# Softmax denominators gathered across four units, with a new written order, in an adaLN attention and token-MLP block

## The chip, the core and the metric

The kernel runs on one core of one Trainium2 chip. The engines that compute are PE (TensorE, matrix multiply into PSUM), DVE (VectorE), ACT (ScalarE) and POOL (GpSimd); SP (SyncE) issues nearly all DMA transfers here. The metric is device microseconds of one execution; a profile is one execution of its own, and its span runs from the first to the last instruction.

## What is computed

Two branches in a row over x (2048 tokens, 512 features), each behind a layer norm that is scaled and shifted by vectors made from a condition c. The first is attention with 32 heads of 16 features, causal, with a window of 256 keys. The second is an MLP that mixes tokens.

```python
mod = (_silu(c) @ w_mod).reshape(c.shape[0], 6, 1, -1)
sa, ca, ga, sb, cb, gb = (mod[:, i] for i in range(6))
h = _layernorm(x, axis=-1) * (1 + ca) + sa
x = x + ga * _A_ref(h, A_wqkv, A_wo)        # softmax(q k / 4, mask) v, then wo
h = _layernorm(x, axis=-1) * (1 + cb) + sb
x = x + gb * _B_ref(h, B_w1, B_b1, B_w2, B_b2)
# _B_ref: layernorm, gelu(w1^T h + b1) over tokens, then w2^T u + b2
```

## The kernel before

**Groups, units and chunks.** The 2048 tokens are worked in four groups G of 512, each of four tiles of 128. A *unit* is one set of eight heads (g8, of four) for 256 queries (H, of eight): 32 units. Their score blocks are packed into 75 *chunks*. A chunk is four strips of 512 columns: the score matmul S writes three strips to the PSUM tile `pss`, of which there is one, and one to `psb`, of which there are two; ACT takes two exponentials from them, the large EA (`et<-pss`, 128x1536) and the small EB (`et<-psb`, 128x512); DVE multiplies by the mask (M). When the last chunk of a unit is masked, the matmuls AV make values (`po[:,0]`) and, by a matrix of ones, sums (`po[:,1]`) in one PSUM bank. Each sum stands in the 16 partitions of its head. Groups 0 to 3 begin at chunks 0, 15, 35 and 55.

**After a unit** (`finish`, L1265): ACT takes the logarithm of the sums out of PSUM (ln), then the exponential of minus that (rz), both 128x256 and both into the tile `lz`; DVE multiplies values from PSUM by it into `OT`. The bank is free when that product is done.

**Work between the chunks.** Three PSUM banks ("od") are shared by AV and by all dense matmuls, which come in pieces of two 128x512 products: projections q, k, v of the next group (`proj`), the output projection wo, residual and second norm of the group before (`post`), and the first MLP product (`partials`: p for the first eight token tiles, p2 for four of them added later). ACT, DVE or POOL take the results out: ke, qe, ve copy projections from PSUM, kk, vo, vp lay out keys and values, n2, m2, hb make the second norm, pe and pd keep partial sums. When attention is over, `tail` ends the first MLP product (56 pieces u), with gelu (g), and last come 16 output tiles (`py`) of 14 products each.

**Order.** All of this is a list of 1165 operations. `ORDER` (L62) lists their numbers in the order in which they are written into the program, and so into each engine's queue; `CHOSEN` (L118) names the engine of those that can run on several. Each engine and SP work through their own queue in that order and wait for what an instruction needs. The costs in the code, such as 0.26 for ln, belong to the planner that made the order; the chip doesn't see them.

**DMAs in the middle.** SP issues xt (a transposing transfer of a normed tile into `h1T`, four to a group), vx (two transfers that swap halves of the values, `vs<-vb`), z2 (zeros for `VT`), and the weight loads w1a to w1d and w2, among others.

```python
ea = op("EA", "ACT", ..., deps=[s] + readers.get(i - E_BUFS, []), pos=i, cls="exp")
a = op("ln", "ACT", 0.26, e_ln, deps=[av], pos=i + LZ_POS)
b = op("rz", "ACT", 0.31, e_rz, deps=[a], pos=i + LZ_POS)
d = mult_ops[Hh, g8] = op("OT", "DVE", 0.34, e_o, deps=[b], pos=i + OT_POS)
unit["avs"][0].frees = [d]
```

Of the kernel before, what the change touches and what calls it, by code (L numbers as in the profile page):

```python
# [10 lines left out]
ALU = mybir.AluOpType  # L11
# [5 lines left out]
H = 32  # L17
# [42 lines left out]
E_BUFS = 7  # L60
LOG = None
ORDER = [  # L62
# [54 lines left out]
]  # L117
CHOSEN = {  # L118
    "ACT": [
        47, 48, 50, 51, 74, 82, 1062,  # L120
    ],
    "DVE": [
# [5 lines left out]
    ],  # L128
    "POOL": [
# [4 lines left out]
    ],  # L134
}
BATCH = True
XT_AFTER = -0.7
W1_AFTER = 2.0
AV_POS = 0.2
LZ_POS = 0.0  # L140
# [75 lines left out]
def kernel(  # L216
# [31 lines left out]
    class Ordered:  # L248
        def __init__(self, engine):
            self.engine = engine  # L250
# [1184 lines left out]
```

## Time and profile before

| | us |
|---|---|
| median of three runs | 253.65 (252.9 to 253.68) |
| span of the profiled execution | 252.3 |
| busy in it: PE, DVE, ACT, POOL | 235.3, 205.4, 179.5, 126.3 |
| granted TensorE clock, mean | 1.000 |

Nearly every operation is recorded at L256, the line of the wrapper that calls the engine, so groups are told apart by their tiles, not by lines. A row of groups gives count, busy time in us and mean duration in ns of one. ACT and DVE instructions overlap a little, so an instruction's duration is longer than its share of a full queue; that share is read from start to start. A table by stretches gives busy us and count of each engine.

### The profile page before, as it was taken

What the parts mean: (1) busy time and instruction counts of PE and PEld (TensorE: products, weight loads), DVE (VectorE), ACT (ScalarE), POOL (GpSimd) and SP (SyncE); (2) the same over time, 40 slices, a digit from 0 to 9 for tenths busy, and PEclk for the clock granted to TensorE, in tenths of its full rate; (3) what the DMA queues carried; (4) which work ended last, traced back from release to release, by engine and by line L of the source; (5) the groups of instructions that cost most, each with busy time, mean ns of one, the idle gap of its engine ahead of it and who ended that gap; (6) DMA issues with size and microseconds to landing.
All of it is one profiled execution on the core that took longest, in us unless ns stands there. A gap on an engine that the chain in (4) does not pass through costs nothing.

```text
span 252.3 us, 9189 instructions
## 1 busy us (share of the span) xinstructions
PE 235.3 (93%) x3949; PEld 126.0 (50%) x3949; DVE 205.4 (81%) x408; ACT 179.5 (71%) x254; POOL 126.3 (50%) x228
## 2 busy tenths in 40 slices
PE   7988888899987889999999999999999999999995
PEld 2656644445554544555546454556444444444443
DVE  5499998989989998999897999999978764444443
ACT  4699998999999999999999999997147510000000
POOL 8268968795899989845886348173000000000000
PEclk9999999999999999999999999999999999999999
DMA  6999364356055200003401536314999201111111
GB/s 200 323 351 294 48 47 86 44 70 187 3 74 112 53 23 3 4 3 104 131 3 45 155 82 189 105 44 113 343 388 386 108 22 43 44 52 52 42 44 42
DMA packets 42625, 28.13 MB, mean 111 GB/s; under 512 B 12376, under 2 KB 38488, under 8 KB 42584
## 3 DMA queue, kind: packets, MB, share of 16 engines
q1 hardware_dynamic: 42576, 27.54, 39.4%
q8 instruction: 31, 0.51, 0.9%
q14 instruction: 10, 0.08, 0.1%
q10 hardware_dynamic: 8, 0.00, 0.0%
HBM read 22.03 MB, written 2.10 MB: 96 GB/s over the span
## 4 chain that ended last, share of the span: by engine, by line
PE 52%; ACT 24%; DVE 7%; DMA 5%; issue 5%; POOL 4%; SPq 1%; POOLq 0%; DVEq 0%
ACT et L256 20%; PE py L256 19%; PE pu L256 16%; PE po L256 5%; PE pss L256 5%; ACT lz L256 3%; PE pa L256 3%; DMA x<-in_A_x_dram 2%; DVE et L256 2%; DMA h1T<-xn 2%; DMA wmod<-in_w_mod_dram 1%; POOL h1T L256 1%; PE pq L256 1%; DVE st L256 1%; PE pk L256 1%
## 5 line engine op out<-in xcount | busy, mean ns | idle before, releaser
L256 ACT ACTIVATE et<-pss 128x1536 bf16<-128x1536 f32 x75 | 110.7, 1476 | 2.8 <-PE psb L256 2.3
L256 PE MATMUL py<-guT,w2r 128*128 128x512 bf16 (+2 forms) x238 | 48.7, 366 | 0.0
L256 ACT ACTIVATE et<-psb 128x512 bf16<-128x512 f32 x75 | 46.9, 626 | 0.0
L256 DVE TENSOR_TENSOR et<-et,maskt 128x1024 bf16<-128x1024 bf16 (+2 forms) x79 | 46.4, 603 | 0.1
L256 PE MATMUL pu<-hb,w1s 128*32 128x512 bf16 (+1 forms) x302 | 39.0, 380 | 0.2 <-DVE QT L256 0.2
L256 PEld LDWEIGHTS <-w2r 128*128 128x128 bf16 x238 | 22.8, 98 | 26.1 <-issue 0.3
L256 PE MATMUL pss<-QT,KT 32*128 32x64 bf16 (+3 forms) x720 | 29.9, 230 | 6.2 <-ACT et L256 3.5
L256 PE MATMUL po<-et,VT 128*32 128x64 bf16 (+3 forms) x960 | 32.2, 234 | 1.3 <-DVE kb L256 0.6
L256 PE MATMUL po<-et,ones_bd 128*32 128x256 bf16 (+3 forms) x624 | 31.7, 268 | 0.0
L256 PEld LDWEIGHTS <-KT 32*128 32x128 bf16 x960 | 17.1, 92 | 28.5 <-issue 24.6
L256 DVE TENSOR_TENSOR otile<-py,xr 128x512 bf16<-128x512 f32 (+2 forms) x17 | 11.2, 660 | 24.4 <-PE py L256 24.2
L256 POOL TENSOR_SCALAR KT<-kb,mask_par 128x512 bf16<-128x512 bf16 (+1 forms) x36 | 25.0, 707 | 11.4 <-DVE kb L256 11.1
L256 PE MATMUL psb<-QT,KT 32*128 32x64 bf16 (+3 forms) x240 | 29.3, 231 | 0.0
L256 PEld LDWEIGHTS <-VT 128*32 128x32 bf16 x960 | 20.8, 96 | 13.2 <-issue 4.7
L256 PE MATMUL pk<-h1T,wqkv 128*32 128x512 bf16 (+4 forms) x228 | 21.1, 340 | 2.4 <-DVE OT L256 1.0
L256 DVE BATCH_NORM_STATS2 st<-x 128x6 f32<-128x512 bf16 x32 | 21.5, 680 | 2.1 <-DMA x<-in_A_x_dram 2.1
L256 PEld LDWEIGHTS <-wqkv 128*32 128x32 bf16 (+1 forms) x350 | 15.3, 96 | 12.7 <-issue 4.7
L256 PEld LDWEIGHTS <-w1s 128*32 128x32 bf16 (+1 forms) x302 | 14.1, 97 | 15.0 <-issue 1.5
L256 PE MATMUL pv<-wqkv,h1T 128*32 128x512 bf16 (+2 forms) x202 | 17.1, 348 | 1.3 <-DVE OT L256 0.7
L256 PE MATMUL pu<-hb,w1r 128*128 128x512 bf16 (+1 forms) x96 | 17.9, 380 | 0.0
L256 PE MATMUL pa<-wod,OT 128*32 128x512 bf16 (+1 forms) x136 | 17.2, 381 | 0.0
L256 PEld LDWEIGHTS <-ones_bd 128*32 128x32 bf16 x624 | 15.8, 97 | 0.1
(109 smaller groups left out, 350.1 us busy)
## 6 DMA issues: line engine op xcount, KB each, us to landing
w2r<-in_B_w_dram SPq DMA_DIRECT2D x14, 512.0 KB, 10.2
w1s<-in_B_w_dram SPq DMA_DIRECT2D x19, 256.0 KB, 4.0
w1r<-in_B_w_dram SPq DMA_DIRECT2D x9, 256.0 KB, 4.3
x<-in_A_x_dram SPq DMA_DIRECT2D x16, 128.0 KB, 5.2
wmod<-in_w_mod_dram SPq DMA_DIRECT2D x4, 512.0 KB, 7.8
out_dram<-otile SPq DMA_DIRECT2D x15, 128.0 KB, 1.7
wmod<-in_w_mod_dram SPq DMA_DIRECT2D x4, 256.0 KB, 3.9
wqkv<-in_A_wqkv_dram SPq DMA_DIRECT2D x4, 256.0 KB, 5.7
```

Source lines behind the costliest of these rows:

```text
L256: ins = call(*args, **kwargs)
```

## The change

**Sums (`finish`).** For 30 of the 32 units, values and sums are copied together from PSUM to an SBUF tile `ev` (128x512, f32, six of them) by DVE (26) or ACT (4); this copy frees the bank. A DMA (zg) then takes every eighth partition of the sums, 16 rows, to `zc`, where four units (two in the last batch) lie under one another. One ln and one rz, at most 64x256, serve the batch. A DMA for each unit (zb) spreads its 16 rows back over the 128 partitions of `ev`, and POOL (25) or DVE (5) multiplies values by it into `OT`. The last two units go as before, their lz in `ev`.

**Condition vectors.** The four vectors bc were made by 16 matmuls with 128 identical rows and taken out by four DVE instructions. Now 16 matmuls of 32 columns go side by side into one bank, one DVE instruction takes them out, and four DMAs (bb) spread them over the partitions.

**Written order.** On every engine each recorded instruction depends (without a semaphore) on the one before it, so none can change places where a pool is opened or closed. `ORDER` and `CHOSEN` are new, for 1206 operations; up to the first chunk the sequence is that of before with other numbers.

**Memory.** `et` has six buffers, not seven; the `work` pool is gone and its tiles are in `wpool`; `nothing` is in `modw`; the last four `hb` tiles are made after `wpool` is closed, and wait for it. Some costs of the planner are changed.

Counted by the numbers in the two orders, operations on each engine:

| | before | after |
|---|---|---|
| ln + rz on ACT | 32 + 32 | 10 + 10 |
| ev on DVE / ACT | none | 26 / 4 |
| OT on DVE / POOL | 32 / 0 | 7 / 25 |
| ve on DVE / ACT | 16 / 0 | 13 / 3 |
| pe on DVE / ACT | 13 / 1 | 10 / 4 |
| kk on DVE / POOL | 1 / 18 | 3 / 16 |
| vo on DVE / POOL | 2 / 10 | 0 / 12 |
| zg, zb, bb on SP | none | 30, 30, 4 |

```diff
-E_BUFS = 7
+E_BUFS = 6
+EV_BUFS = 6
 ORDER = [
...
                 if pinned[0]:
                     tc.keep_in_program_order(ins)
+                    if self.last is not None:
+                        tc.add_manual_dep(
+                            ins.ins, self.last, mybir.DependencyInfo(mybir.DependencyClass.NoSync, mybir.DependencyReason.DATA),
+                            reason="order",
+                        )
+                    self.last = ins.ins.name
...
+    def e_bc(n):
+        if n == 0:
+            box["bc"] = bank([P, D], F32, "ps_b")
+        for k in (2 * n, 2 * n + 1):
+            for i, (v, _) in enumerate(vectors):
                 te.matmul(
-                    box["bc", v][:], lhsT=sT_rep[:, k, :], rhs=wmod[:, k, v * D : (v + 1) * D],
-                    start=(k == 0), stop=(k == ND - 1),
+                    box["bc"][32 * i : 32 * i + 32, :], lhsT=sT_rep[:, k, :], rhs=wmod[:, k, v * D : (v + 1) * D],
+                    start=(k == 0), stop=(k == ND - 1), tile_position=(0, 32 * i), skip_group_check=True,
                 )
...
+    bce = op("bce", "DVE", 0.6, e_bce, deps=[bc_last], pos=9.0)
+    for n, (v, dst) in enumerate(vectors):
+        def e_bb(e, n=n, dst=dst):
+            dma.dma_start(out=dst[:], in_=bcs[32 * n : 32 * n + 32, :].unsqueeze(1).to_broadcast([32, ND, D]))
...
+        def e_ev(e):
+            e_new()
+            copy(e, unit["ev"][:], unit["ps"][:])
+
+        def e_zg(e):
+            dma.dma_start(out=zc[rows, :], in_=unit["ev"][0 : P : P // DH, 1, :])
+
+        def e_zb(e):
+            dma.dma_start(out=unit["ev"][:, 1, :], in_=zc[rows, :].unsqueeze(1).to_broadcast([DH, P // DH, HQ]))
+
+        a = op("ev", {"DVE": 0.6, "ACT": 0.5}, 0.6, e_ev, deps=[av], pos=i + LZ_POS)
+        unit["avs"][0].frees = [a]
+        g = op("zg", "SP", 0.56, e_zg, deps=[a], pos=i + LZ_POS, extra=-0.2)
+        members.append((unit, i, tag, a, g, e_o, e_zb))
+        if len(members) < (2 if Hh == 2 * NG - 1 else 4):
+            return
...
+        a = op("ln", "ACT", 0.26, e_bln, deps=[m[4] for m in members], pos=i + LZ_POS)
+        b = op("rz", "ACT", 0.31, e_brz, deps=[a], pos=i + LZ_POS)
+        for u, at, tag, first, g, e_mult, e_spread in members:
+            z = op("zb", "SP", 0.6, e_spread, deps=[b], pos=at + LZ_POS, extra=1.1)
+            d = mult_ops[u["H"], u["g8"]] = op("OT", {"DVE": 0.34, "POOL": 0.66}, 0.34, e_mult, deps=[z], pos=at + OT_POS)
```

More of the change, by code (lines that the diff above doesn't have):

```diff
@@ L250, in __init__ @@
             self.engine = engine
+            self.last = None
         def __getattr__(self, name):
@@ L274 @@
     xres = [xpool.tile([P, D], BF, name=f"x{t}") for t in range(NT)]
-    hb = [xpool.tile([P, D], BF, name=f"hb{t}") for t in range(NT)]
+    hb = [xpool.tile([P, D], BF, name=f"hb{t}") for t in range(NT - ND)]
     identity = const.tile([P, P], BF, name="identity")
@@ L300 @@
     wod = const.tile([P, ND, D], BF, name="wod")
+    zc = const.tile([P, HQ], F32, name="zc")
     maskt = const.tile([P, 3, KB], BF, name="maskt")
@@ L306 @@
     nc.gpsimd.memset(ones_bd[KB:P, DH : 2 * DH], ZSCALE)
-    nothing = const.tile([P, D], BF, name="nothing")
-    nc.vector.memset(nothing[:], 0.0)
     late = ctx.enter_context(tc.tile_pool(name="late", bufs=2))
@@ L335 @@
     modw = tc.alloc_tile_pool(name="modw", bufs=1, side="right")
-    warm = nothing
+    warm = nothing = modw.tile([P, D], BF, name="nothing")
+    nc.vector.memset(nothing[:], 0.0)
     wmod = modw.tile([P, ND, 6 * D], BF, name="wmod")
@@ L473 @@
     sT = modw.tile([P, ND], BF, name="sT")
-    sT_rep = modw.tile([P, ND, P], BF, name="sT_rep")
+    sT_rep = modw.tile([P, ND, 32], BF, name="sT_rep")
+    bcs = modw.tile([P, D], BF, name="bcs")
+    bc_fix = modw.tile([P, 2], F32, name="bc_fix")
+    nc.gpsimd.memset(bc_fix[:, 0:1], 1.0)
+    nc.gpsimd.memset(bc_fix[0:32, 0:1], ZSCALE)
+    nc.gpsimd.memset(bc_fix[:, 1:2], 0.0)
+    nc.gpsimd.memset(bc_fix[32:64, 1:2], 1.0)
     box = {}
@@ L504 @@
     o5.frees = [o6]
-    o_rep = op("sTrep", "DVE", 0.35, lambda e: ve.tensor_copy(
-        out=sT_rep[:], in_=sT[:].unsqueeze(2).to_broadcast([P, ND, P])), deps=[o6], pos=-6, ready=15.0)
+    o_rep = op("sTrep", "DVE", 0.15, lambda e: ve.tensor_copy(
+        out=sT_rep[:], in_=sT[:].unsqueeze(2).to_broadcast([P, ND, 32])), deps=[o6], pos=-6, ready=15.0)
     def e_fm(k):
@@ L610, in norm_ops @@
         if quiet:
-            return op(f"{tag}ag", "POOL", 3.1, e_ag, deps=st_ops, pos=poss[-1])
+            return op(f"{tag}ag", "POOL", 3.3, e_ag, deps=st_ops, pos=poss[-1])
         return op(f"{tag}rs", "ACT", 0.45, e_rs, deps=st_ops, pos=poss[-1])
@@ L781, in e_kb @@
             def e_kb(e):
-                box["kb", g8] = work.tile([P, D], BF, name="kb", tag=kb_tag, bufs=1)
+                box["kb", g8] = wpool.tile([P, D], BF, name="kb", tag=kb_tag, bufs=1)
                 copy(e, box["kb", g8][:, 0 : 2 * P], box["kq", g8][:, 0, :])
@@ L823, in e_ve @@
             def e_ve(e):
-                box["vb", tb] = work.tile([P, 2, 256], BF, name="vb", tag=vb_tag, bufs=1)
+                box["vb", tb] = wpool.tile([P, 2, 256], BF, name="vb", tag=vb_tag, bufs=1)
                 copy(e, box["vb", tb][:], box["v", tb][:])
@@ L953, in e_ke @@
                 else:
-                    box["kb", g8] = work.tile([P, D], BF, name="kb", tag=kb_tag, bufs=1)
+                    box["kb", g8] = wpool.tile([P, D], BF, name="kb", tag=kb_tag, bufs=1)
                     copy(e, box["kb", g8][:], box["k", g8][:])
@@ L982, in e_ve @@
             def e_ve(e):
-                vb = box["vb", tb] = work.tile([P, 2, 256], BF, name="vb", tag=vb_tag, bufs=1)
+                vb = box["vb", tb] = wpool.tile([P, 2, 256], BF, name="vb", tag=vb_tag, bufs=1)
                 copy(
@@ L989, in e_vx @@
             def e_vx(e):
-                vs = box["vs", tb] = work.tile([P, 256], BF, name="vs", tag=vs_tag, bufs=1)
+                vs = box["vs", tb] = wpool.tile([P, 256], BF, name="vs", tag=vs_tag, bufs=1)
                 dma.dma_start(out=vs[0:KB, :], in_=box["vb", tb][KB:P, 0, :])
@@ L1045, in post @@
             a.frees = [x_ops[tl]]
-        engine, shifted = ({"POOL": 0.77, "DVE": 0.35}, True) if G < POOL_POST else ({"DVE": 0.34}, False)
+        engine, shifted = ({"POOL": 0.74, "DVE": 0.33}, True) if G < POOL_POST else ({"DVE": 0.34}, False)
         st = norm_ops("l2", lambda i: xres[4 * G + own[i]], [[x_ops[tl]] for tl in own],
@@ L1062, in post @@
             n_ops.append(op("n2", engine, 0.33, e_n, deps=[st], pos=at(0.4 + 0.32 * j / n)))
-            h_ops.append(op("m2", {"DVE": 0.74, "POOL": 2.5} if G < NG - 1 else "DVE", 0.74, e_m, deps=n_ops[-1:], pos=at(0.43 + 0.32 * j / n)))
+            h_ops.append(op("m2", {"DVE": 0.80, "POOL": 2.1} if G < NG - 1 else "DVE", 0.80, e_m, deps=n_ops[-1:], pos=at(0.43 + 0.32 * j / n)))
         st = norm_ops("l3", lambda i: h2[own[i]], [[o] for o in h_ops],
@@ L1096, in load @@
             name = f"w1{'abcd'[quarter]}"
-            o = loads[pair, quarter] = op(name, "SP", 1.3, lambda e: load_w1(pair, quarter), deps=deps, pos=pos, extra=W1_AFTER)
+            o = loads[pair, quarter] = op(name, "SP", 0.55, lambda e: load_w1(pair, quarter), deps=deps, pos=pos, extra=W1_AFTER)
             return o
@@ L1102, in e_rel @@
             box["B"] = ctx.enter_context(tc.tile_pool(name="partB", bufs=1, side="right"))
+            hb.extend(box["B"].tile([P, D], BF, name=f"hb{t}") for t in range(NT - ND, NT))
         for n in range(NF // 2):
@@ L1267, in finish @@
         av = av_ops[G, g8] = unit["avs"][-1]
-        lz_tag = turn("lz")
-        def e_ln(e):
-            unit["lz"] = late.tile([P, HQ], F32, name="lz", tag=lz_tag, bufs=1)
-            ac.activation(out=unit["lz"][:], in_=unit["ps"][:, 1, :], func=ACT.Ln)
-        def e_rz(e):
-            ac.activation(out=unit["lz"][:], in_=unit["lz"][:], func=ACT.Exp, scale=-1.0)
+        tag = turn("ev", EV_BUFS)
+        direct = Hh == 2 * NG - 1 and g8 >= 2
+        members = box.setdefault("batch", [])
@@ L1277, in e_o, with e_new @@
+        def e_new():
+            unit["ev"] = kvpool.tile([P, 2, HQ], F32, name="ev", tag=tag, bufs=1)
         def e_o(e):
-            ve.tensor_tensor(
+            ENGINE[e].tensor_tensor(
                 out=OT[G % 2][g8][:, (Hh % 2) * HQ : (Hh % 2 + 1) * HQ],
-                in0=unit["ps"][:, 0, :], in1=unit["lz"][:], op=ALU.mult,
+                in0=(unit["ps"] if direct else unit["ev"])[:, 0, :], in1=unit["ev"][:, 1, :], op=ALU.mult,
             )
-        a = op("ln", "ACT", 0.26, e_ln, deps=[av], pos=i + LZ_POS)
@@ L1284, in finish, with e_ln, e_rz @@
-        b = op("rz", "ACT", 0.31, e_rz, deps=[a], pos=i + LZ_POS)
-        d = mult_ops[Hh, g8] = op("OT", "DVE", 0.34, e_o, deps=[b], pos=i + OT_POS)
-        unit["avs"][0].frees = [d]
-        slot(lz_tag, a, d)
+        if direct:
+            def e_ln(e):
+                e_new()
+                ac.activation(out=unit["ev"][:, 1, :], in_=unit["ps"][:, 1, :], func=ACT.Ln)
+            def e_rz(e):
+                ac.activation(out=unit["ev"][:, 1, :], in_=unit["ev"][:, 1, :], func=ACT.Exp, scale=-1.0)
+            a = op("ln", "ACT", 0.26, e_ln, deps=[av], pos=i + LZ_POS)
+            b = op("rz", "ACT", 0.31, e_rz, deps=[a], pos=i + LZ_POS)
+            d = mult_ops[Hh, g8] = op("OT", "DVE", 0.34, e_o, deps=[b], pos=i + OT_POS)
+            unit["avs"][0].frees = [d]
+            slot(tag, a, d)
+            return
@@ new lines, in finish @@
+        base = KB * (box.setdefault("batches", 0) % 2)
+        rows = slice(base + DH * len(members), base + DH * len(members) + DH)
+        def e_ev(e):
+            e_new()
+            copy(e, unit["ev"][:], unit["ps"][:])
[4 more added lines that the diff above has]
+        a = op("ev", {"DVE": 0.6, "ACT": 0.5}, 0.6, e_ev, deps=[av], pos=i + LZ_POS)
@@ new lines, in finish, with e_bln, e_brz @@
+        unit["avs"][0].frees = [a]
+        g = op("zg", "SP", 0.56, e_zg, deps=[a], pos=i + LZ_POS, extra=-0.2)
+        members.append((unit, i, tag, a, g, e_o, e_zb))
+        if len(members) < (2 if Hh == 2 * NG - 1 else 4):
+            return
+        own = slice(base, base + DH * len(members))
+        def e_bln(e):
+            ac.activation(out=zc[own, :], in_=zc[own, :], func=ACT.Ln)
+        def e_brz(e):
+            ac.activation(out=zc[own, :], in_=zc[own, :], func=ACT.Exp, scale=-1.0)
@@ new lines, in finish @@
+        n = box["batches"]
+        a = op("ln", "ACT", 0.26, e_bln, deps=[m[4] for m in members], pos=i + LZ_POS)
+        for m in members:
+            m[4].deps.extend(tenants.get(f"zc{n % 2}", []))
+        b = op("rz", "ACT", 0.31, e_brz, deps=[a], pos=i + LZ_POS)
+        spread = []
+        for u, at, tag, first, g, e_mult, e_spread in members:
+            z = op("zb", "SP", 0.6, e_spread, deps=[b], pos=at + LZ_POS, extra=1.1)
+            spread.append(z)
+            d = mult_ops[u["H"], u["g8"]] = op("OT", {"DVE": 0.34, "POOL": 0.66}, 0.34, e_mult, deps=[z], pos=at + OT_POS)
+            slot(tag, first, d)
@@ L1289 @@
+        tenants[f"zc{n % 2}"] = spread
+        box["batches"] += 1
+        box["batch"] = []
     for G in range(NG):
```

50 lines of the change are left out of this document (22 added, 28 removed), and 128 rows, old and new, of tables (CHOSEN, ORDER).

## The prediction, made before the changed kernel ran

> **What bounds the kernel now.** I read the page first, then a table by stretches, then the timeline of ACT, SP and POOL where a term needed a price.
>
> ```profile
> span 252.3 us, 9189 instructions
> PE 235.3 (93%) x3949; PEld 126.0 (50%) x3949; DVE 205.4 (81%) x408; ACT 179.5 (71%) x254; POOL 126.3 (50%) x228
> PE 52%; ACT 24%; DVE 7%; DMA 5%; issue 5%; POOL 4%; SPq 1%; POOLq 0%; DVEq 0%
> ```
>
> The averages hide the stages. I cut the span where the large exponentials of chunks 0, 15, 35, 55 and 70 start (11.22, 44.57, 87.60, 129.53, 162.03 us; first and last quoted below), then at the end of attention and at the start of the output tiles:
>
> ```profile
> 11.22:44.57 33.35, 28.73 (x632) 18.86 (x632) 31.43 (x70) 32.25 (x44) 25.57 (x45) 1.00 0.71 171
> 44.57:87.60 43.03, 38.16 (x966) 21.42 (x969) 40.84 (x80) 42.23 (x59) 36.78 (x60) 1.00 0.41 80
> 87.60:129.53 41.93, 39.83 (x901) 21.72 (x895) 38.95 (x72) 41.80 (x56) 32.30 (x57) 1.00 0.15 41
> 129.53:162.03 32.50, 32.07 (x681) 17.02 (x680) 29.60 (x54) 32.15 (x45) 17.74 (x29) 1.00 0.41 112
> 11.22:162.03 150.81, 138.79 (x3171) 79.02 (x3171) 140.82 (x273) 148.43 (x201) 112.41 (x190) 1.00 0.40 96
> 175.00:200.80 25.80, 25.80 (x121) 11.65 (x120) 22.11 (x52) 11.52 (x21) 0.00 (x0) 1.00 0.89 315
> 200.80:252.30 51.50, 48.69 (x239) 22.65 (x237) 24.23 (x39) 1.84 (x3) 0.00 (x0) 1.00 0.12 42
> ```
>
> The columns are stretch, its length, then busy us of PE, PEld, DVE, ACT and POOL. Over 70 chunks ACT is busy 148.4 of 150.8 us and DVE 140.8 (93%); PE has 12.0 us free, nearly all before 129.5 us. From 129.5 us on PE has almost nothing free. So ACT and, close behind, DVE set the pace early; PE sets the end.
>
> Per chunk there is also a floor:
>
> ```profile
> 11.22 1.45 ACT L256 ACTIVATE et<-pss 128x1536 bf16<-128x1536 f32 x1 [0.73 <-PE psb L256]
> 16.53 1.45 ACT L256 ACTIVATE et<-pss 128x1536 bf16<-128x1536 f32 x1
> 18.47 1.45 ACT L256 ACTIVATE et<-pss 128x1536 bf16<-128x1536 f32 x1
> 162.03 1.48 ACT L256 ACTIVATE et<-pss 128x1536 bf16<-128x1536 f32 x1
> ```
>
> With no ln or rz between them, large exponentials follow 1.94 us apart, because the one `pss` is read, refilled and read again. The mean is 150.81 / 70 = 2.15, so at most 70 x 0.21 = 15 us could go by relieving ACT.
>
> **What the change takes from ACT.** Prices from start to start in a full queue:
>
> ```profile
> 46.38 0.41 ACT L256 ACTIVATE lz<-po 128x256 f32<-128x256 f32 x1
> 46.64 1.48 ACT L256 ACTIVATE et<-pss 128x1536 bf16<-128x1536 f32 x1
> 47.97 0.46 ACT L256 ACTIVATE lz<-lz 128x256 f32<-128x256 f32 x1
> 48.28 0.64 ACT L256 ACTIVATE et<-psb 128x512 bf16<-128x512 f32 x1
> 48.76 1.50 ACT L256 ACTIVATE et<-pss 128x1536 bf16<-128x1536 f32 x1
> ```
>
> ln takes 0.26, rz 0.31, a copy of 512 columns as much as the small exponential, 0.48. Counting the two orders, ln/rz fall in the four stages from 5/5, 9/8, 7/8, 7/7 to 1/1, 2/2, 2/2, 2/2. ACT gains three ve and loses about one short copy in the first (+1.5), one ke in the third (+0.5), three ev in the fourth (+1.5). So ACT loses 0.8, 3.7, 2.7 and 1.4 us: 8.6 of 150.8. The batch's ln waits for a DMA, and behind it stand the next exponentials; in the order the last batch has EA, EB, EA (3.2 us) between its last ACT copy and ln, where a gather's issue and landing take about 2.5 (prices below). Others have more, so I put this wait at nothing; each us late would cost up to one us, eight times.
>
> **What it puts on DVE.**
>
> ```profile
> L256 DVE TENSOR_TENSOR OT<-po,lz 128x256 bf16<-128x256 f32 x32 | 13.2, 415 | 2.4 <-ACT lz L256 1.9
> L256 DVE COPY part<-pu 128x512 f32<-128x512 f32 x13 | 8.8, 678 | 0.3 <-PE pu L256 0.2
> L256 DVE TENSOR_SCALAR bc_ga<-ps_b 128x512 bf16<-128x512 f32 x1 | 0.7, 665 | 0.0
> ```
>
> The 26 copies ev have the shape of the row `part<-pu`: 26 x 0.678 = 17.6. Taken away: 25 products at 0.415 = 10.4, three of the four bc copies (2.0), and seven ve, pe and qe that go to ACT (4.7). In the second stage, say: ev +9 (6.1), OT -7 (-2.9), ke, n2, vp, wod, l1st +6 (+3.2), l3st, m2, qe, ve, vo, xn -10 (-6.4), in all +0.1 with rounding. The four stages change by +0.3, +0.1, -0.3 and +2.3 us: DVE is not relieved, its 140.8 become 143.2. So what ACT gives up is worth only what DVE can pack denser. It was 93.4% busy over the 70 chunks, 94.9% in its best stage (40.84 of 43.03), and 99.3% in its best ten us:
>
> ```profile
> 160.00:170.00 10.00, 10.00 (x186) 5.02 (x187) 9.93 (x21) 9.87 (x14) 4.23 (x8) 1.00 0.11 31
> ```
>
> These are the bounds: at 94.9% the 70 chunks take 143.2 / 0.949 = 150.9 us, no gain, and at 99.5%, with hardly a gap, 143.9. I take 97.5%, near the middle, since copies now free banks without waiting for ln and rz: 146.9 us, **3.9 shorter**. That is above the floor of 70 x 1.94 = 135.8, and within ACT's relief.
>
> **What it does on PE.** A piece of dense work takes 0.43 (below, 16 matmuls, two pieces, in 0.86 from start to start). The vectors bc were 8 pieces, 3.4 us; in four column strips side by side they take a quarter, 0.86: 2.6 less, in the first stage, where PE waits anyway. After chunk 70 the new order holds seven more pieces and three fewer AV (0.34 each): +2.0 us in a stretch where PE is never idle. So the sum is -3.9 + 2.0 = **-1.9 us**. PE's own account agrees: it loses 2.6 us of work, and its free 12.0 us grow by 0.7.
>
> ```profile
> 170.66 1.04 PE L256 MATMUL pu<-hb,w1s 128*32 128x512 bf16 x16
> 171.52 1.04 PE L256 MATMUL pu<-hb,w1r 128*32 128x512 bf16 x16
> ```
>
> **What hides the DMAs.** SP gets 64 more.
>
> ```profile
> vs<-vb SPq DMA_DIRECT2D x24, 32.0 KB, 1.9
> w1s<-in_B_w_dram SPq DMA_DIRECT2D x19, 256.0 KB, 4.0
> 44.89 1.14 SPq L256 DMA_DIRECT2D vs<-vb  x2
> 50.42 4.85 SPq L256 DMA_TRANSPOSE h1T<-xn  x3
> 175.02 13.69 SPq L256 DMA_DIRECT2D w2r<-in_B_w_dram  x14
> ```
>
> One small issue takes 0.57, a transposing one up to 1.6. In chunks 15 to 34 SP's own time rises from some 22 to 35 us of 42; it still has room, but a gather that waits for its copy now holds back vx and xt, for which POOL's vp and h1T wait. A gather (16 KB) should land like vs, in 1.9; a spread (128 KB) between vs and a w1 load, 1.9 to 4.0, and I take 3. The products come a group's length before wo needs them, except at the end. That w2 is issued after more w1 loads costs nothing: it goes out at 175.0, PE then has 25.8 us of other work, and the order moves it by about 3.
>
> **POOL** takes 25 products.
>
> ```profile
> L256 POOL TENSOR_TENSOR h<-h,bc_cb 128x512 bf16<-128x512 bf16 x4 | 5.3, 1328 | 4.1 <-DVE h L256 4.0
> L256 DVE TENSOR_TENSOR h<-h,bc_cb 128x512 bf16<-128x512 bf16 x12 | 5.4, 448 | 0.9 <-POOL h L256 0.8
> L256 DVE TENSOR_TENSOR et<-et,maskt 128x1024 bf16<-128x1024 bf16 (+2 forms) x79 | 46.4, 603 | 0.1
> ```
>
> Half of 1.328 is 0.66 for 256 columns. [...] That makes 25 x 0.66 = 16.5 us more on POOL; its other moves nearly cancel.
>
> [...]
>
> **Sum and clock time.** 252.3 - 1.9 = 250.4 of span. The median of the runs lies 1.35 above this execution's span, and I keep that distance: **251.7**. A measurement here can tell about 0.3%, 0.76 us: faster is below 252.9, slower above 254.4.
>
> **Rivals.**
> 1. *DVE packs fully.* At 99.5% the 70 chunks take 143.9: -6.9 + 2.0 = -4.9, time **248.7**. For it: banks come free earlier, and PE now waits for DVE's product, which waits for rz (the rows below). Against it: three engines would run without gaps.
> 2. *The last pair's round trip stops PE.* Gather 1.9, ln and rz 0.57, two issues 1.1, spread 1.9 to 4.0, product 0.66: 6.1 to 8.2 us. Between the last gather and wo of tile 2 the order gives PE 14 pieces, six AV and one S: 14 x 0.43 + 6 x 0.34 + 0.23 = 8.3. One w1 load is ahead of one spread; two us late gives **253.7**, no change.
> 3. *DVE gets no denser (slower).* Its copies wait for PE, its masks for ACT as now, so it stays at the 94.9% of its best stage: 0 + 2.0, time **255.7**. It decides from the point where DVE stays under 96.2%, at which 143.2 us take 148.8 and pay just for the 2.0. For it: DVE was so dense beside an ACT that was full too. Against it: ACT, which it waited for, loses 8.6.
> 4. *POOL's queue becomes the bound.* In chunks 15 to 34 POOL gets 10 products (6.6), kk +2 (2.8), vo +2, vp -1, xn +1, n2 -1 (+1.0): 36.8 + 10.4 = 47.2 us, where the stage lasted 43.0. Products that wait for spreads stand ahead of xn, h1T, kk and vp of the next group; what is late is then the first scores of group 2, and ACT. Price: 47.2 - 42.0 = 5.2 us, and **256.9**. Against it: the five chunks behind have only 3.8 us of POOL work, and the most urgent kk stand early.
> [...]
> 6. *The dependency changes nothing.* SP's issues of before already follow the written order, so this edit alone has no price.
>
> ```profile
> DVE OT L256 <- ACT lz L256: 1.9, 4, 0.8
> PE pk L256 <- DVE OT L256: 1.0, 1, 1.0
> PE pv L256 <- DVE OT L256: 0.7, 1, 0.7
> L256 POOL TENSOR_SCALAR KT<-kb,mask_par 128x512 bf16<-128x512 bf16 (+1 forms) x36 | 25.0, 707 | 11.4 <-DVE kb L256 11.1
> L256 POOL COPY VT<-vs 64x256 bf16<-64x256 bf16 x24 | 10.8, 452 | 3.9 <-DMA vs<-vb 3.0
> ```
>
> **Chances.** Forecast 0.33, the first five rivals 0.19, 0.12, 0.16, 0.13 and 0.07. Faster: 0.19 and 0.30 of the forecast's, 0.49. Same: 0.03 of the forecast's, most of the second, some of the third, 0.15. Slower: 0.36. The forecast's own range is 250.2 to 253.2 (DVE at 98.5% and 96.5%). The range for 8 in 10 reaches from 248.7 to 256.9, since cases of both signs hold most of the chance.
>
> **What would show it.** Right: ev near 0.68 us, OT on POOL near 0.7, ACT's ln never idle in wait of a DMA, DVE over 96% busy to chunk 70, which starts 3 to 5 us earlier than 162.0, PE never idle from there. Wrong: gaps on ACT before et or lz that a DMA or POOL ends, POOL above 95% busy in chunks 15 to 40, masks above 0.65 us, or PE idle before the last output projection.

## The result, and the profile after

The changed kernel takes 273.98 us (median of four runs, 269.74 to 274.84) against 253.67 us: a ratio of 1.0707 with an interval of 1.0632 to 1.0782. (The ratio leaves disturbed runs out, so it stands for 271.6 us; where differences between kernels are taken below, they are differences of ratios, and one per cent is 2.54 us.) The forecast of 251.7 us had the wrong sign, and the time lies far above its range. The profiled execution took 273.26 us. Its page, in three lines:

```profile
span 271.6 us, 8953 instructions
PE 242.9 (89%) x3757; PEld 128.8 (47%) x3757; DVE 219.2 (81%) x401; ACT 177.0 (65%) x221; POOL 148.8 (55%) x255
PEclk9999979997999959999989999989999999999999
```

PE has 192 matmuls fewer, since in the new order 64 products fewer are cut into four strips of columns, and is busy 7.6 us longer. The third line gives the reason for part of it: some slices have a granted clock of 0.5 to 0.8; before, all were 9.

The stages of after, cut as before at the exponentials of chunks 0, 15, 35, 55, 70 and 74 and at the first output tile (length, then busy us of PE, PEld, DVE, ACT and POOL):

```profile
12.57:45.51 32.94, 29.05 (x656) 19.38 (x658) 30.97 (x69) 31.50 (x39) 26.44 (x47) 0.95 0.72 167
45.51:92.23 46.72, 39.77 (x854) 21.61 (x850) 39.39 (x73) 40.11 (x45) 40.06 (x63) 0.96 0.53 101
92.23:137.44 45.21, 38.58 (x866) 21.38 (x859) 44.40 (x71) 40.46 (x46) 34.69 (x55) 0.92 0.29 58
137.44:173.82 36.38, 33.15 (x677) 18.12 (x677) 34.72 (x57) 31.93 (x38) 25.67 (x42) 0.95 0.38 91
173.82:188.20 14.38, 11.43 (x153) 5.16 (x152) 12.67 (x19) 9.47 (x13) 11.59 (x18) 0.88 0.46 107
188.20:220.18 31.98, 31.77 (x241) 15.14 (x239) 26.86 (x62) 16.66 (x31) 3.10 (x4) 1.00 0.97 313
12.57:173.82 161.25, 140.55 (x3045) 80.48 (x3044) 149.47 (x266) 143.99 (x165) 126.86 (x204) 0.95 0.47 100
```

Against before the first four stages differ by -0.4, +3.7, +3.3 and +3.9 us; chunks 70 to 74 took 8.3 us (162.0 to 170.3) and take 14.4, +6.1; the stretch behind them +1.5 (30.5 to 32.0), the output tiles -0.1; and chunk 0 starts 1.35 later. The sum is the 19.3 us of the two spans. The late start need not come from the change: two kernels below that differ from the new one only behind chunk 15 start chunk 0 at 11.35 and at 13.34 us. DVE is busy 149.47 us over the 70 chunks, not 143.2, and that is 92.7% of them, not 97.5%. ACT, at 98% before, is down to 89%, so its relief is real; it only waits now. PE's free time before chunk 70 grew from 12.0 to 20.7 us.

The groups that changed (count, busy us, mean ns), in the order masks, copies, modulation on DVE, then products and modulation on POOL:

```profile
L260 DVE TENSOR_TENSOR et<-et,maskt 128x1024 bf16<-128x1024 bf16 (+2 forms) x79 | 52.2, 684 | 1.8 <-ACT et L260 1.8
L260 DVE COPY ev<-po 128x512 f32<-128x512 f32 x26 | 17.4, 679 | 1.7 <-issue 1.0 <-POOL OT L260 0.6
L260 DVE TENSOR_TENSOR h<-h,bc_sb 128x512 bf16<-128x512 bf16 x11 | 8.2, 747 | 0.4
L260 DVE TENSOR_TENSOR h<-h,bc_cb 128x512 bf16<-128x512 bf16 x11 | 7.4, 672 | 0.0
L260 POOL TENSOR_TENSOR OT<-ev 128x256 bf16<-128x256 f32 x25 | 20.2, 818 | 7.6 <-DMA ev<-zc 7.2
L260 POOL TENSOR_TENSOR h<-h,bc_sb 128x512 bf16<-128x512 bf16 x5 | 7.1, 1414 | 0.4
L260 POOL TENSOR_TENSOR h<-h,bc_cb 128x512 bf16<-128x512 bf16 x5 | 6.2, 1236 | 0.3
```

ev came as forecast (678 expected, 679 found). But instructions that the change did not touch became longer: masks from 603 to 684 ns (79 x 0.081 = 6.4 us), DVE's h by bc_cb from 448 to 672 (11 x 0.224 = 2.5), its h by bc_sb from 500 to 747 (11 x 0.247 = 2.7). These 11.6 us are more than the 6.3 by which DVE's load misses the forecast.

What lengthens them is seen in the timeline of after, all lines of DVE and POOL from 171.9 to 177.0 us, around chunk 70 (start, duration):

```profile
171.94 1.16 POOL L260 TENSOR_TENSOR h<-h,bc_cb 128x512 bf16<-128x512 bf16 x1
172.13 1.25 DVE L260 TENSOR_TENSOR h<-h,bc_cb 128x512 bf16<-128x512 bf16 x1
173.18 1.22 POOL L260 TENSOR_TENSOR h<-h,bc_sb 128x512 bf16<-128x512 bf16 x1
173.41 1.26 DVE L260 TENSOR_TENSOR h<-h,bc_sb 128x512 bf16<-128x512 bf16 x1
174.38 1.19 POOL L260 TENSOR_SCALAR h<-x,rs,nm 128x512 bf16<-128x512 bf16 x1
174.59 0.41 DVE L260 TENSOR_TENSOR h<-h,bc_cb 128x512 bf16<-128x512 bf16 x1
175.04 0.80 DVE L260 TENSOR_TENSOR h<-h,bc_sb 128x512 bf16<-128x512 bf16 x1
175.65 1.21 POOL L260 TENSOR_TENSOR h<-h,bc_cb 128x512 bf16<-128x512 bf16 x1
175.76 2.93 DVE L260 TENSOR_TENSOR et<-et,maskt 128x1024 bf16<-128x1024 bf16 x2
176.94 1.48 POOL L260 TENSOR_TENSOR h<-h,bc_sb 128x512 bf16<-128x512 bf16 x1
```

The same DVE instruction takes 1.25 us in the first pair and 0.41 at 174.59. In the first pair it ends 0.28 us behind POOL's: 172.13 + 1.25 = 173.38 against 171.94 + 1.16 = 173.10; the next pair ends 0.27 apart. At 174.59 POOL is not idle either. There it is POOL's normalization, with one tensor input, that is longer: it takes 1.19 us, where undisturbed ones (at 87.0 and 130.6 us) take 0.77, and the next product of DVE (175.04) ends 0.27 us behind it. Two masks took 2.93 us, each 0.68 where nothing meets it.

Over the whole trace, the 11 masks that share 0.2 us or more with a product `OT` or a modulation on POOL take 1188 ns on average, the 66 that share nothing with them 599. DVE's 22 modulation instructions fall in two kinds: eight take 0.41 to 0.43 us, and 14 end 0.27 to 0.28 us behind an instruction of POOL, ten of them behind one with two tensor inputs, four behind one with a single one. In the old kernel five of 24 end so, four of them behind a single input. So DVE's two-input work ends behind POOL's normalizations, copies and key layouts, with one input, too (in after at 175.04, 141.61 and 99.33 us); what the new kernel adds is longer instructions, in worse places.

In the two pairs above DVE's instruction is the second to start. The traces show that it ends behind POOL's, not why.

Where these late masks tell, and what else waits (us in total, times, longest):

```profile
ACT et L260 <- PE psb L260: 14.6, 10, 3.7
PE pss L260 <- ACT et L260: 8.7, 16, 2.1
POOL OT L260 <- DMA ev<-zc: 7.2, 5, 3.1
```

PE's wait in front of `pss` was 3.5 us before. Behind its waits stands the second loss: POOL's products wait for their spreads in POOL's own queue, and what stands behind them there is late. The chain that ended last shows it in chunks 24 to 34 (start, us, what):

```profile
74.64 1.38 POOL OT L260 x2
76.02 2.50 POOL xn L260 x2
...
83.27 4.16 DMA h1T<-xn
87.56 0.56 DVE h1T L260 x2
```

Products go ahead of the normalizations xn of the next group. SP begins to issue the four transposes at 78.54 us, in the old kernel at 72.51, and takes no longer for them (6.0 us against 6.7). The last land after 4.2 us, and the masks of chunk 35 stand behind h1T. From chunk 34 to 35 it takes 4.9 us instead of 2.2.

### The profile page after: what moved, and what is told of

Read it like the earlier page. It is cut to its first block, busy times and chain, and to the rows that moved or that the text cites. A ratio compares the mean times of both kernels' runs of the same rounds, so it can differ in the third digit from the quotient of the medians.

```text
span 271.6 us, 8953 instructions
## 1 busy us (share of the span) xinstructions
PE 242.9 (89%) x3757; PEld 128.8 (47%) x3757; DVE 219.2 (81%) x401; ACT 177.0 (65%) x221; POOL 148.8 (55%) x255
## 4 chain that ended last, share of the span: by engine, by line
PE 47%; DVE 15%; ACT 6%; DMA 5%; POOL 3%; SPq 2%; issue 2%; DVEq 0%; ACTq 0%; POOLq 0%
PE py L260 18%; PE pu L260 13%; PE po L260 7%; ACT et L260 6%; DVE et L260 5%; PE pss L260 4%; DVE h L260 4%; PE pa L260 2%; DMA w1s<-in_B_w_dram 2%; SPq L260 2%; DVE ev L260 2%; PE pv L260 2%; PE pq L260 2%; DMA h1T<-xn 2%; POOL xn L260 1%
## 5 line engine op out<-in xcount | busy, mean ns | idle before, releaser
L260 ACT ACTIVATE et<-pss 128x1536 bf16<-128x1536 f32 x75 | 108.8, 1450 | 17.3 <-PE psb L260 14.6
L260 DVE TENSOR_TENSOR et<-et,maskt 128x1024 bf16<-128x1024 bf16 (+2 forms) x79 | 52.2, 684 | 1.8 <-ACT et L260 1.8
L260 ACT ACTIVATE et<-psb 128x512 bf16<-128x512 f32 x75 | 44.6, 594 | 0.1
L260 PE MATMUL pu<-hb,w1s 128*128 128x512 bf16 (+1 forms) x206 | 39.5, 391 | 2.3 <-DVE part L260 2.1
L260 PE MATMUL po<-et,VT 128*32 128x64 bf16 (+3 forms) x960 | 34.2, 245 | 7.0 <-DVE part L260 2.9
L260 PEld LDWEIGHTS <-VT 128*32 128x32 bf16 x960 | 23.0, 101 | 17.3 <-issue 12.2
L260 POOL TENSOR_TENSOR OT<-ev 128x256 bf16<-128x256 f32 x25 | 20.2, 818 | 7.6 <-DMA ev<-zc 7.2
L260 PEld LDWEIGHTS <-w1s 128*128 128x128 bf16 (+1 forms) x206 | 14.1, 98 | 20.0 <-issue 4.8
L260 PEld LDWEIGHTS <-wqkv 128*32 128x32 bf16 (+1 forms) x326 | 14.9, 99 | 12.8 <-issue 5.4
L260 DVE COPY ev<-po 128x512 f32<-128x512 f32 x26 | 17.4, 679 | 1.7 <-issue 1.0
L260 PE MATMUL pu<-hb,w1r 128*128 128x512 bf16 x72 | 18.2, 382 | 0.0
```

The lines of the kernel that those rows point to most:

```text
L260: ins = call(*args, **kwargs)
```

## The experiments

Four theories were put to the chip: POOL's new products and VectorE's two-input work hold each other up (the expectations call this the shared interface, or the interface; the name is a conjecture of the author's, and no run shows what the two engines share); SP's queue with the new transfers holds other transfers back; the products' waits for the spreads hold POOL's queue; or the new order itself makes the loss. The first four kernels take the new sums apart, each of the first three on top of the one before.

**The wait for the spreads.** The product takes the values twice, so that it waits for no spread; left out is the division by the sums.

```diff
-                in0=(unit["ps"] if direct else unit["ev"])[:, 0, :], in1=unit["ev"][:, 1, :], op=ALU.mult,
+                in0=(unit["ps"] if direct else unit["ev"])[:, 0, :], in1=unit["ev"][:, 1 if direct else 0, :], op=ALU.mult,
```

> The changed kernel, but the 30 products read values twice instead of values and spread sums, so they wait for their copy only; gathers, batch ln and rz, and spreads still run. The division by the sums is left out. If products that wait for spreads hold up POOL's queue (its idle time in wait of spreads is 7.2 us in the changed kernel), the time falls from 274 by 5 to 12 us, to 262 to 269. If the loss comes from a full SP queue, from POOL and DVE slowing each other, or from the new order, it stays within 3 us of 274.

269.22 us, ratio 1.0586 (1.0510 to 1.0661): 3.1 us less than the new kernel, with intervals that overlap a little. POOL's product is 715 ns, masks stay at 689.

**No gathers and spreads at all.** On top of that, both transfers of each unit are left out.

```diff
-            dma.dma_start(out=zc[rows, :], in_=unit["ev"][0 : P : P // DH, 1, :])
+            pass
...
-            dma.dma_start(out=unit["ev"][:, 1, :], in_=zc[rows, :].unsqueeze(1).to_broadcast([DH, P // DH, HQ]))
+            pass
```

> As the run before, and no gathers or spreads at all: SP issues 60 transfers fewer, and the batch ln and rz work on a constant without a wait. The sums are left out of the output. If SP's queue is the cause (in chunks 15 to 34 its transfers take 35.8 of 46.7 us, and xt and vx come late behind gathers), the time falls to 255 to 262 and ACT's waits for PE from 14.6 us to under 6. If POOL and DVE slow each other, it stays above 266, with masks still near 0.68 us and the DVE products by bc_sb near 0.75.

267.26 us, 1.0525 (1.0465 to 1.0585). Not told apart from the run before it by time; in its trace chunks 15 to 34 take 41.1 us, where the run before needs 45.2 and the new kernel 46.7. SP's queue as the one cause would have given far more: transfers and waits together are some 4.6 of the 17.9 us.

**Short products.** On top of that, 32 of 256 columns of each product.

> As the run before, and the products take 32 of 256 columns; the other columns of OT stay zero. If POOL's products slow DVE's instructions with two SBUF inputs, masks go back from 0.684 to about 0.60 us and the DVE products by bc_sb from 0.747 to about 0.50, and the time falls by 6 to 12 us against the run before. If not, masks stay and the time falls by less than 3 us.

262.78 us, 1.0306 (1.0247 to 1.0365): 5.6 us less, a little under the 6 to 12 expected. Masks fall to 628 ns and DVE's h by bc_sb from 732 to 664, not to 500. Chunk 70 starts at 161.9 us, level with the old kernel; chunks 70 to 74 still take 14.4.

**The new order with the sums as before** (ln, rz and product of each unit where its copy stood; no batches).

> The new written order with the sums as before: at the place of each copy ev stand ln and rz on ACT and the product on DVE, out of PSUM; gathers, batches, spreads and later products are empty. The condition vectors stay in strips. If the way of the sums makes the loss, this is 252 to 258 us. If the new order, the strips or the dependency make it, it stays above 264.

284.79 us, 1.1206 (1.1144 to 1.1268). It tells only that the new way of sums is not worse than the old one in this order: the order was laid out for engines without that work, so this does not measure the order alone.

**Spare products in the old kernel.** 28 instructions on POOL that nobody waits for, one at each unit's end, with two inputs, and as a control with one.

```diff
+            if Hh < 2 * NG - 1:
+                nc.gpsimd.tensor_tensor(out=spill[:, 0, :], in0=spare[:], in1=spare[:], op=ALU.mult)
```

> The kernel before, to which GpSimd's queue gets 28 more products of 128x256 float elements with two inputs from SBUF, one at each unit's end, that nothing waits for (their output is not used). No order, transfer or wait of the old kernel is changed. If GpSimd's two-input products lengthen VectorE's two-input work (theory of the shared interface): masks of 128x512 and 128x1024 together from 603 ns to 640-690 ns, VectorE 4 to 8 us busier before chunk 70, and 257-263 us in all. If only the new order and the SP queue make the loss: masks within 600-615 ns and 253-255.5 us.

> The same with one-input work: 28 instructions of GpSimd on 128x2x216 elements with one input from SBUF and two scalars, of about the length of the products (0.8 us each expected). Shared interface: masks within 600-625 ns and 253-256 us, well below the kernel with two inputs. If it is GpSimd's queue that is full, whatever it runs: as slow as the kernel with two inputs, within 1.5 us.

275.62 us (1.0578 to 1.0835) and 277.16 us (1.0735 to 1.0923): some 18 and 21 us longer, and no test of the first theory. The timeline of POOL in the kernel with two inputs shows why:

```profile
9.89 11.74 POOL L1286 TENSOR_TENSOR spill<-spare 128x256 bf16<-128x256 f32 x17
```

The spare work had no input to wait for and was written past the recorder that holds the others in order, so 17 products ran in one block in front of the key layout (KT, at 21.6 us) that the first chunks wait for. By 29.8 us all 28 were done, and none stood beside a mask. What it measures is a POOL queue that is blocked at the start.

**The condition vectors alone.** The old kernel with its four vectors in column strips, all four transfers issued where the first vector's copy stood; then the same with each transfer where its own vector's copy stood.

```diff
-            for i, d in enumerate((bc_ga, bc_cb1, bc_sb, bc_gb)):
-                dma.dma_start(out=d[:], in_=bcs[32 * i : 32 * i + 32, :].unsqueeze(1).to_broadcast([32, ND, D]))
+            i, d = {2: (0, bc_ga), 4: (1, bc_cb1), 3: (2, bc_sb), 5: (3, bc_gb)}[v]
+            dma.dma_start(out=d[:], in_=bcs[32 * i : 32 * i + 32, :].unsqueeze(1).to_broadcast([32, ND, D]))
```

> The kernel before with one part of the change: the four condition vectors as column strips of one bank, one copy and four transfers in place of four banks and four copies. TensorE loses some 2.6 us of work and VectorE some 2 us, all before chunk 15. If that work lies on the path: 250.5-252.8 us. If it is hidden there: 253-254.5 us.

> The kernel before with the condition vectors in column strips, as in the run at 256.6 us, but each of the four transfers issued where the vector's copy stood (chunks 7, 10, 10 and 11) instead of all four at chunk 7, in between the transposes of the second group's input. If those four transfers in SP's queue made the strips slower than before: 251.5-253.8 us. If the strips cost for another reason (their copy, the order on TensorE): 255.5-257.5 us.

256.64 us, 1.0075 (1.0034 to 1.0116), and 254.72 us, 1.0032 (1.0004 to 1.0060). The four issues in a row took SP 2.6 us in the middle of the transposes of group 1:

```profile
28.25 0.69 SPq L256 DMA_DIRECT2D bc_ga<-bcs  x1
...
30.27 0.61 SPq L256 DMA_DIRECT2D bc_gb<-bcs  x1
```

The first stage takes 35.0 us in this trace, 33.1 with the issues placed apart and 33.4 in the old kernel. The two times differ by 0.43%, which their intervals do not tell apart, and both lie outside the ranges expected. In neither are the 2.6 us of PE and 2 us of DVE that the strips save worth anything: that work was hidden. No version here beats the old kernel.

**The second modulation on VectorE** in the new kernel: all of it, then only the pair at chunk 70.

```diff
+    choice.update({i: "DVE" for i in choice if ops[i].name == "m2"})
...
+    choice[738] = "DVE"
```

> The new kernel with the two-input products of the second modulation (h by bc_cb, h by bc_sb) all on VectorE. VectorE gets some 1 us more for each that moves. Shared interface: the two masks that took 1.64 and 1.37 us at chunks 70 and 71 fall to 0.7-0.9 us, TensorE's stall of 2.95 us and the slow clock behind it go, chunks 70 to 74 take 10-12.5 us instead of 14.4, and the whole 268.5-272 us against 274.0. If the stall is the order's and not the interface's: 13.5-15 us there and 273-277 us.

> The new kernel with a single pair of two-input products (h by bc_cb and bc_sb of the tile that GpSimd has at chunk 70) on VectorE, nothing else moved. Shared interface: the two masks of 1.64 and 1.37 us fall below 1 us each, the stall of 2.95 us in front of the value matmuls shrinks below 1.5 us, chunks 70 to 74 take 11-13 us instead of 14.4 and the whole 270.5-272.8 us. If VectorE's own queue makes that stall: 14-16 us there, 273.5-276 us in all.

278.93 us (1.0828 to 1.1007) and 277.10 us (1.0814 to 1.0979), both outside the times expected. Chunks 70 to 74 did fall to 10.0 and 10.7 us, as the first theory has it, but the time came back in front of them: with the single pair moved, DVE stood 5.4 us in its queue until POOL had normalized that tile, and PE 5.4 us behind it.

**One-input products**, in the kernel without gathers and spreads: two scalings of 256 and 64 columns in place of each product.

> The new kernel without gathers and spreads (its run: 267.3 us, masks 676 ns, the product 715 ns on GpSimd) in which GpSimd's products are one-input scalings of the value half, in two pieces of 256 and 64 columns, so that GpSimd is kept for about the product's own time, 0.65-0.75 us together; what is left out is the product with the reciprocal sums. Shared interface, with two inputs as its condition: masks fall to 630-650 ns and the time to 262.5-265.5 us, near the 262.8 us of the kernel with short products. If what costs is the time that GpSimd's queue is kept: masks may fall, the time stays at 266-269 us.

266.18 us, 1.0486 (1.0416 to 1.0555), not told apart from 1.0525. POOL was kept 0.77 us per unit (2 x 0.387, from its group) instead of 0.71. Masks fell from 676 to 644 ns. So of the 5.6 us that short products gave, this run does not say how much is the second input and how much POOL's time; the last experiment comes back to this.

**All products on VectorE**, with the transfers and without.

> The new kernel with all products of the gathered units on VectorE and none on GpSimd. VectorE gets 25 products of some 0.35 us (8.8 us), loses what GpSimd's products put on its masks and modulations (6 to 9 us), and GpSimd loses 20 us. If GpSimd's chain of products, copies and normalizations is what holds the new order: 266-271 us. If VectorE's own load is: 272-277 us. If nothing of either: 280 us or more.

> The new kernel without gathers and spreads (its run: 267.3 us) and with its products of values by values on VectorE, so that GpSimd has none and no product waits for a transfer. VectorE gets 25 products of 0.35 to 0.45 us (9 to 11 us) and gets back what GpSimd's two-input products put on it in that run (masks from 676 to 605-615 ns, 5 us; modulations 4 to 5 us). If GpSimd's time with the products is what costs: 259-264 us. If VectorE's load is, whoever lays it on: 265-270 us. That the 296.1 us of the run with all products on VectorE came from VectorE's waits for the spreads (25.6 us in its trace) shows in either case: below 272 us.

296.06 us (1.1602 to 1.1724) and 271.87 us (1.0666 to 1.0734). In the first, masks are back at 607 ns, and the time is lost in a wait:

```profile
DVE OT L261 <- DMA ev<-zc: 25.6, 8, 5.8
```

The second, without that wait, shows that VectorE is the worse place even so: its 30 products take 555 ns each, 16.4 us, and the whole is 4.4 us slower than with products on POOL (1.0525). VectorE's load would explain that, but the time lies above the 265 to 270 us expected for it, so this is not shown.

**No products, then short copies as well**, on top of the kernel with short products; the second cuts the copies ev to 32 columns of each half.

> The kernel with short products (262.8 us) without any product of the gathered units, on either engine; left out are gathers, spreads and products, the logarithms and exps of the batches stay. Masks fall from 628 to 605-620 ns. If the rest of the loss still is the products and the interface: 255-260 us. If it is the new order after chunk 35 (TensorE's work moved behind chunk 70, the modulation on GpSimd there): 261-263 us, with chunks 70 to 74 still at 13.5-15 us.

> As the kernel without products, and the copies of both halves to SBUF cut from 256 to 32 columns each, 27 of them on VectorE, which loses about 0.5 us on each (13 us), 4 on ScalarE. If VectorE's load bounds the new order's chunks: 4 to 8 us less than the kernel without products. If the order does (who stands behind whom): less than 2 us.

265.49 us (1.0409 to 1.0526) and 265.81 us (1.0404 to 1.0514). The first lies above both its ranges. There is no gain from either, though DVE's copies went from 17.6 to 5.5 us in the second. That rules out products, transfers and the copies as the cause of the 11.6 us that stay (4.6%). The kernel without products is even slower than the one with short ones (1.0306): its h by bc_sb on DVE rose from 664 to 754 ns, and the six modulation instructions of DVE that stand beside POOL's took 1196 ns instead of 990, so the modulations met more closely.

**The added dependency.**

> The new kernel without the added dependency of each transfer on the one before: on SP's queue nine weight loads then stand one to three places earlier, no other engine's instructions change. If the dependency is no part of the loss: 272-275.5 us against 274.0. If holding those loads back costs: 268-271.5 us.

275.08 us, 1.0820 (1.0752 to 1.0888): no part of the loss, since the time without it is no shorter.

**One input in place of two in POOL's modulations.** Two scalings of 512 and 128 columns in place of each product with bc_cb and bc_sb on POOL, five tiles in all; first on the kernel with short copies, then on the new kernel alone. Left out is the modulation of these five tiles.

```diff
+                if e == "POOL":
+                    for width in (D, D // 4, D, D // 4):
+                        nc.gpsimd.tensor_scalar(
+                            out=u[:, 0:width], in0=u[:, 0:width], scalar1=0.5, scalar2=0.0, op0=ALU.mult, op1=ALU.add,
+                        )
+                    return
```

> The kernel without products and with short copies (265.8 us), where GpSimd's five pairs of modulation products (h by bc_cb, h plus bc_sb, two inputs from SBUF) are one-input scalings of 512 and 128 columns each, about as long on GpSimd; left out is the modulation of these five tiles. If the two-input products beside VectorE's make the stalls at chunks 37, 55 and 71: the masks there fall to 0.7 us, h by bc_sb on VectorE from 754 to below 520 ns, the stalls of 2.1 and 2.97 us below 1 us and the time to 258-262 us. If the order makes them whatever GpSimd does: 263.5-267 us.

> The same edit alone in the new kernel (274.0 us), its products, gathers and spreads kept. Interface: 267.5-271.5 us, chunks 70 to 74 in 11-13 us instead of 14.4, masks from 684 to 640-660 ns. Order: 272.5-275.5 us.

256.00 us, 1.0087 (1.0058 to 1.0116), and 266.70 us, 1.0498 (1.0460 to 1.0536): 9.4 us less than the kernel with short copies, 5.3 us less than the new kernel. Both are as the first theory expected, or better. First the kernel with short copies, then the same with one-input modulations; stages 55 to 70 and 70 to 74, and DVE's groups:

```profile
132.20:167.70 35.50, 32.43 (x671) 17.71 (x675) 31.09 (x55) 31.01 (x38) 19.77 (x35) 0.95 0.26 72
167.70:182.50 14.80, 11.49 (x152) 5.29 (x154) 12.78 (x18) 9.35 (x14) 10.10 (x16) 0.88 0.46 124
```

```profile
130.90:163.50 32.60, 31.05 (x671) 16.94 (x675) 29.56 (x55) 30.97 (x38) 17.59 (x35) 1.00 0.27 78
163.50:173.60 10.10, 9.89 (x154) 4.94 (x155) 9.54 (x17) 9.37 (x15) 7.69 (x16) 1.00 0.66 181
```

```profile
L260 DVE TENSOR_TENSOR h<-h,bc_sb 128x512 bf16<-128x512 bf16 x11 | 8.3, 754 | 0.4
L260 DVE TENSOR_TENSOR h<-h,bc_cb 128x512 bf16<-128x512 bf16 x11 | 7.2, 652 | 0.0
```

```profile
L260 DVE TENSOR_TENSOR h<-h,bc_cb 128x512 bf16<-128x512 bf16 x11 | 6.2, 567 | 0.0
L260 DVE TENSOR_TENSOR h<-h,bc_sb 128x512 bf16<-128x512 bf16 x11 | 5.8, 527 | 0.4
L1083 POOL TENSOR_SCALAR h<-h 128x512 bf16<-128x512 bf16 (+1 forms) x20 | 10.5, 537 | 0.9
```

With the same order and nearly the same counts, and POOL kept 10.5 us instead of 12.8, chunks 55 to 74 get 7.6 us shorter, and the granted clock there is 1.00 again. DVE itself is only 4.8 us less busy in these chunks; PE is 4.6 us less idle, and busy 3.0 us less for nearly the same counts, where its granted clock had been 0.95 and 0.88. The times alone do not tell the second input from the shorter instruction: a scaling of 512 columns keeps POOL 0.62 us where it is undisturbed, a product 1.16. The traces do. With one input DVE still ends behind POOL: in the first of these kernels six of DVE's modulation instructions end 0.27 to 0.28 us behind a scaling. But DVE's 22 are shorter, 547 ns on average instead of 703. So the gain goes with POOL's shorter instructions; a second input on POOL is not needed for DVE's to end behind them.

## Why the prediction was wrong

**The account.** By ratio the new kernel loses 17.9 us. Without wait, transfers and seven eighths of the products it loses 7.8, so these make about 10; the modulations make 5.3 (in the new kernel) to 9.4 (in the one with short copies), and 2.2 us stay open (the profiled execution, the slowest of eight, starts chunk 0 2.5 us late). The shares do not add up exactly, since the modulations meet more closely when the products are gone.

**DVE's load and density: the step that failed.** The forecast's gain rests on "143.2" and "97.5%", and both were wrong: DVE was busy 149.5 us before chunk 70, at 92.7%. Load: the same instructions were priced by their group means of before, and 11.6 us of lengthening came on top (above). Against undisturbed instructions, masks and modulation lost 5.4 us before chunk 70 in the old kernel and 14.0 in the new: 8.6 more, where the load missed by 6.3. Density: it fell below the 93.4% of before. The waits for ln and rz, 1.9 us, are gone, but DVE stands 3.1 us in front of h1T at chunk 35 and 2.3 us in front of a projection of values.

**The fifth of the chances, 0.07,** was for POOL's 25 products lengthening DVE's masks. They do (masks fell from 676 to 628 ns with short products), but what weighs most is the modulation: POOL has five pairs instead of four, which "its other moves nearly cancel" passed over, and the new order lays them beside DVE's own. Against 0.41 and 0.68 us of undisturbed masks (512 and 1024 columns) and 0.42 of undisturbed modulation, those on DVE that share 0.2 us or more with POOL's modulations are 7.6 us longer in sum, those that share it with its products alone 4.6. In the new kernel 11 of DVE's modulation instructions share 0.2 us or more with a two-input instruction of POOL; in the old one, one does. The group means of before hide all this. Single rows of before show it, beside one input and beside two (DVE and POOL in two timelines of before):

```profile
72.30 1.79 POOL L256 TENSOR_SCALAR h<-x,rs,nm 128x512 bf16<-128x512 bf16 x2
...
73.56 0.80 DVE L256 TENSOR_TENSOR h<-h,bc_sb 128x512 bf16<-128x512 bf16 x1
74.07 0.93 POOL L256 TENSOR_SCALAR xn<-x,rs,nm 128x512 bf16<-128x512 bf16 x1
...
74.62 0.93 DVE L256 TENSOR_TENSOR et<-et,maskt 128x1024 bf16<-128x1024 bf16 x1
...
79.17 1.15 POOL L256 TENSOR_TENSOR h<-h,bc_sb 128x512 bf16<-128x512 bf16 x1
...
79.80 0.80 DVE L256 TENSOR_TENSOR h<-h,bc_cb 128x512 bf16<-128x512 bf16 x1
```

The modulation takes 0.80 us there, where its group means are 448 and 500 ns, and the mask 0.93 instead of 0.68. Of the old kernel's 79 masks 23 end behind an instruction of POOL like this, 0.27 us behind it at 512 columns and 0.54 at 1024. I had weighed this by shares of busy time instead of by the places where the new order puts the two.

**POOL's product at 0.66 us** is 0.82, and 0.71 to 0.72 in the runs whose product reads the values twice, with the transfers or without; 25 x 0.16 = 4 us more on POOL.

**SP "still has room"** held for its share of time and failed for its order. The chain of waits above shows products, then xn, then the transposes that SP issues, and chunk 35 late. Rival 4 had named what is queued behind the products, at 5.2 us; chunks 15 to 34 lost 3.7, and without transfers and waits nothing (41.1 us against 43.0).

**The batch ln "at nothing"**: ACT waited for gathers in front of one ln, 1.99 us, and PE stood for 2.09 us there. A small miss.

**After chunk 70 "+2.0".** Chunks 70 to 74 lost 6.1 us and the stretch behind them 1.5. PE is busy 91.6 us from chunk 70 to the end instead of 87.5 and idle 6.2 instead of 2.8. The idle part and the slow clock go with POOL's modulations (10.1 us for chunks 70 to 74); about two of the 6.1 us stay, as much as the work that I had counted.

**What was right:** ev's price; the strips' saving hidden in the first stage (254.72 against 253.61 us); the dependency without a price (275.08 us without it); ACT no longer full.

## What to carry to other kernels

Before work is moved to GpSimd, look up in the timeline single instructions of VectorE with two SBUF inputs that already run beside GpSimd's work: here a group's mean (448 and 500 ns before) hid that a 0.4 us product took 0.8 us there, in the new kernel up to 1.37, and the new order brought such pairs together, 11 instead of one, that the edit itself never names. Price a moved instruction by what stands behind it in its queue, not by the free share of that queue. When a removed cost gives nothing, as here with the copies (17.6 us of DVE cut to 5.5, 265.49 and 265.81 us in all), change the neighbour of the stall instead: a shorter stand-in told more than any move of work between engines, since each move also moved a wait.

## What the hardware showed

In the new kernel's trace half speed of PE follows its longer stops, with an exception. After idle gaps of 1.05 and 0.99 us (at 32.2 and 33.7 us), the new kernel's clock records show half speed from 34.4 us on for 3.4 us; in all 20.5 us of its span are at half speed, in stretches of 3.4 us or twice that, and no stretch within the old kernel's, whose largest gap between chunks is 0.98 us. The stretches begin at 34.36, 61.67, 95.80, 140.17 and 181.13 us, whole multiples of 3.41 us apart, and in the 3.41 us ahead of each PE is busy 1.2 to 1.7 us. That is no sure sign: a gap of 2.85 us at 87.3 us, with PE busy 1.6 us in the 3.41 us from 85.56 on, was followed by full speed, so no limit comes out of these figures. Eight products of the MLP on PE in the chain of waits of after, at full and at half clock:

```profile
168.75 1.83 PE pu L260 x8
...
181.77 3.22 PE pu L260 x8
```
